# Two pairs of heads turned on TensorE in f32, with new planned durations and a newly planned order

## The chip, the cores and the metric

The kernel runs on one core of a Trainium2 chip. The metric is the device time of one execution in microseconds (us), the median of several runs.

## The reference, cut to what matters

Inputs: q, k, v of 4 batches x 12 heads x 448 rows x 64, in f32, gains g_q and g_k, and two pairs of weights, 768 x 2048 and 2048 x 768. What is computed:

```python
q_n, k_n = rmsnorm(q, g_q), rmsnorm(k, g_k)
scores = (q_n @ k_n.T) / sqrt(64)
attn = exp(scores - max(scores)); attn = attn / (sum(attn) + 1e-9)
x = (attn @ v)                       # 1792 tokens x 768
h = x @ w_in;  x2 = (h * sigmoid(1.702 * h)) @ w_out
h = x2 @ w_in2; out = (h * clip(h + 3, 0, 6) / 6) @ w_out2
```

## The kernel before, in words

The work goes through four batches of 448 tokens. For each batch, q and k are normalised (`add_norm`), the attention of six pairs of heads is computed (`add_units`), and then come the first in-projection with its gate (`add_in1`) and the first out-projection (`add_out1`). The second projection pair runs at the end over all tokens. The attention of batch b + 1 is interleaved with the in- and out-projection of batch b. Large products are made in f16: an f32 operand is split into a high and a low f16 half (`split`, `parts`: the high half by `scaled`, lines 479, 482 and 485 on ScalarE, VectorE and GpSimd; the low one by `rest`, line 494 on VectorE), and three products of halves are added up.

A pair of heads has seven tiles of 128 x 448 scores. For each tile the scores are made on TensorE (lines 1203, 1206), the row maximum on VectorE (1211), the exponential on ScalarE (1215 scales the maximum, 1216, 1221 scales the sum z), and 1/z on VectorE (1224). Then the probabilities must be turned, so that keys lie on partitions. There are two forms of this:

- Batch 0 (f32): a diagonal matrix of 1/z is made from the identity (`scaled(diag, ...)`, lines 479, 482, 485), four f32 matmuls against it turn and scale the tile into PSUM (`flip`, line 1265), a copy brings it to the arena (1275 on ScalarE or 1276 on VectorE), and P·V is made in f32 (`add_head0`, line 1131).
- Batches 1 to 3 (f16): the tile is scaled by 1/z and split into two halves (lines 479 and 494; with line 509 on GpSimd or 510 on VectorE for some tiles), a DMA transpose brings both halves to the arena (line 1227 on SP's queue), V is loaded and split (`add_pair`, line 1145 for the loads), and P·V is made in f16 (line 1164).

The arena is one piece of SBUF. It holds turned probabilities (10 slots in the f32 form, 12 in the f16 form) and, between two attentions, the raw and normalised q and k of the next batch, two pairs at a time. The halves of q and k go to DRAM (line 1067) and come back transposed (1072). Batch b's probabilities wait until all of batch b's q and k have been stored (`arena_after`). The identity and the diagonals lie in the buffer that later holds the halves of V.

The in-projection (line 1410) needs 18 matmuls per block of 128 of the 2048 columns. Each block is read by a tanh on ScalarE (1455), a product on VectorE (1459), and a split (479, 494) into buffer `gt`; `st` has three buffers and PSUM has four banks for it, the flips (three of them at most), P·V and small sums. The out-projection is at line 1478. The weights of the first pair are decoded and scaled in pieces (`Weight`) beside this.

The order of each engine's queue is not written by hand. `Plan.order` simulates the engines with a planned duration for each operation (`t_pe`, `t_act`, `t_dve`, ... and constants at the `op` calls), ranks, biases for each engine and offsets from `CFG`, and emits the operations in the order in which the simulation starts them. An operation with several `ways` goes to the engine on which it would end first, a bias added. `LATENCY`, `late` and `look` are planned delays and windows. Filling matmuls (line 1959) are put where the simulation sees a long gap on TensorE.

Of the kernel before, what the change touches and what calls it, by code (L numbers as in the profile page):

```python
# [34 lines left out]
    bias=[2580, 340, 2500, 1380, 5660],  # L35
    pw=[847, 1827, 3991690324, 32301064499],
    pn=[78, 1413, 6578, 11344],
    ps=[1104, 851, 1934, 2727],
# [4 lines left out]
    look=[0, 130, 60, 920, 540],  # L43
    off=[-9158, 408922, -29895, 22854, 24586, 19810, -27690, 67476, -181023, 15083, 120686, -34408, -37087, -37194, -689989, -31399, -23083, -347804, 11747, 208998],
    abias=44617,
    cuts=[],
    bias0=[2000, 440, 370, 120, 3040],
    bias1=[8820, 1540, 3900, 3250, 4520],
    dlook=2054,
    warm=9,  # L50
    late=789,
    idle=1000,
    pu=419,
    pmost=5,
    pv=1315,
    early_k=[0, 0, 0, 0],
    beside=0.9,
    own={
# [21 lines left out]
def t_pe(n):  # L80
    return 0.445 * n
# [6 lines left out]
def t_dve(n):  # L88
    return 1.04 * n + 70
# [6 lines left out]
def t_fast(n):  # L96
    return Shared(0.72 * n + 80)


def t_dve_two(n):  # L100
    return Shared(1.04 * n + 150)


def t_dve_rest(n):
    return Shared(1.04 * n + 205)


def t_dve_bits(n):
    return Shared(1.04 * n + 150)
# [6 lines left out]
def t_pool2(n):  # L116
    return Shared(1.5 * n + 380)
# [1889 lines left out]
```

## Time and profile before

| | us |
|---|---|
| median of 3 runs (1145.24 to 1148.97) | 1145.58 |
| profiled execution | 1147.63 |
| its span, first to last instruction | 1145.8 |
| TensorE busy | 1065.3 |
| VectorE busy | 822.5 |
| ScalarE busy | 721.3 |
| GpSimd busy | 365.1 |

Busy times are sums over the span; matmuls overlap in their pipeline, so a group of them is read by its start and end, not by the mean of one.

### The profile page before, as it was taken

Reading aid. Unit: us, or ns where it says so; the run is one execution under the profiler, and the core shown is the slowest. Engines: PE = TensorE matmul, PEld = TensorE weight load, DVE = VectorE, ACT = ScalarE, POOL = GpSimd, SP = SyncE. Lnnn points to the kernel's source line nnn. Section 1 sums busy time; section 2 is a strip of 40 time slices with the busy share of each in tenths; the row PEclk is TensorE's granted clock in tenths of the full one; section 3 lists DMA queues with packets and bytes.
Section 4 is the critical chain, followed back from the end, with each engine's and each line's share of the span. In section 5 each row is a group of like instructions: output and inputs, shape, how many; then the busy total and the mean of one; then the engine's idle time right before and its main releaser. Section 6 shows DMA issues by size and latency. Waiting matters only on the chain. (4 is left out here: it accounts for less than half of the span.)

```text
span 1145.8 us, 18018 instructions
## 1 busy us (share of the span) xinstructions
PE 1065.3 (93%) x6571; PEld 588.7 (51%) x6571; DVE 822.5 (72%) x1445; ACT 721.3 (63%) x1505; POOL 365.1 (32%) x335
## 2 busy tenths in 40 slices
PE   3888964999999999999999999999999999999998
PEld 1566531554554555545555555555555555555555
DVE  7998889998699764797756878594577455935342
ACT  5999758999868996578885646463565132512210
POOL 6764555353156201350001255552132103200000
PEclk9999985999999999999999999999999999999999
DMA  8977578999976997569895327633451151222033
GB/s 239 193 199 192 167 203 212 204 191 222 241 227 187 173 176 155 181 194 166 171 185 154 120 78 264 231 108 120 146 189 55 56 169 40 71 72 98 1 90 104
DMA packets 236712, 178.88 MB, mean 156 GB/s; under 512 B 194896, under 2 KB 220496, under 8 KB 235088
## 3 DMA queue, kind: packets, MB, share of 16 engines
q1 hardware_dynamic: 236624, 177.74, 59.4%
q8 instruction: 51, 0.84, 0.3%
q14 instruction: 37, 0.30, 0.1%
HBM read 97.88 MB, written 34.41 MB: 115 GB/s over the span
## 5 line engine op out<-in xcount | busy, mean ns | idle before, releaser
L1410 PE MATMUL mm<-xt,wa 128*128 128x448 f16 x1152 | 229.5, 357 | 7.0 <-DVE st L1459 6.8
L1478 PE MATMUL mm<-gt,wb 128*128 128x448 f16 x1152 | 226.7, 352 | 0.7 <-DVE wb L494 0.5
L1769 PEld LDWEIGHTS <-gt 128*128 128x128 f16 x1344 | 131.4, 98 | 92.3 <-issue 4.8
L1410 PEld LDWEIGHTS <-wa 128*128 128x128 f16 x1152 | 113.9, 100 | 114.3 <-issue 14.5
L1478 PEld LDWEIGHTS <-wb 128*128 128x128 f16 x1152 | 111.8, 99 | 103.9 <-issue 1.1
L1654 PEld LDWEIGHTS <-xt 128*128 128x128 f16 x1008 | 98.6, 98 | 93.7 <-issue 3.8
L1216 ACT ACTIVATE p<-s,smalls 128x448 f32<-128x448 f32 x168 | 120.7, 720 | 7.5 <-DVE p L494 3.4
L1654 PE MATMUL s<-wa,xt 128*128 128x448 f16 x576 | 114.1, 352 | 2.1 <-DVE st L1669 2.1
L1211 DVE TENSOR_REDUCE smalls<-s 128x2 f32<-128x896 f32 (+1 forms) x96 | 91.5, 963 | 4.1 <-PE s L1206 3.9
L494 DVE SCALAR_TENSOR_TENSOR p<-p,smalls 128x448 f16<-128x448 f32 x108 | 78.1, 752 | 22.4 <-ACT p L479 22.1
L1203 PE MATMUL s<-gt 128*128 128x448 f16 (+1 forms) x192 | 62.2, 370 | 30.2 <-ACT p L1216 28.3
L1654 PE MATMUL mm<-wa,xt 128*128 128x448 f16 x432 | 86.9, 352 | 0.9 <-ACT wb L1676 0.9
L479 ACT ACTIVATE p<-p,smalls 128x448 f16<-128x448 f32 (+2 forms) x120 | 75.8, 666 | 11.7 <-DMA xt<-p 8.6
L1769 PE MATMUL mm<-p,gt 128*128 128x384 f16 x384 | 72.0, 326 | 0.0
L1769 PE MATMUL mm<-gt 128*128 128x384 f16 x372 | 68.2, 326 | 0.0
L1206 PE MATMUL s<-gt 128*128 128x448 f16 (+1 forms) x192 | 61.9, 366 | 0.0
L1769 PE MATMUL s<-p,gt 128*128 128x384 f16 x288 | 56.1, 326 | 2.4 <-ACT wb L1805 1.2
L1769 PE MATMUL s<-gt 128*128 128x384 f16 x300 | 55.9, 326 | 1.0 <-DVE st L1669 0.6
L494 DVE SCALAR_TENSOR_TENSOR gt<-st,smalls,gt 128x448 f16<-128x448 f32 x64 | 52.4, 829 | 6.1 <-ACT gt L479 4.9
L1808 DVE SCALAR_TENSOR_TENSOR wb<-mm,smalls,wb 128x384 f32<-128x384 f32 x47 | 27.0, 611 | 41.0 <-PE mm L1769 41.0
L479 ACT ACTIVATE gt<-st,smalls 128x448 f16<-128x448 f32 x49 | 32.1, 661 | 29.9 <-DVE st L1459 26.2
L1265 PE MATMUL mm<-gt,p 128*128 128x128 f32 x336 | 44.1, 280 | 6.3 <-DVE xt L1276 1.9
(216 smaller groups left out, 1827.4 us busy)
## 6 DMA issues: line engine op xcount, KB each, us to landing
wr<-in_moe_w_in_dram SPq DMA_DIRECT2D x32, 768.0 KB, 4.9
wa<-park_x SPq DMA_DIRECT2D x21, 672.0 KB, 4.0
wr<-in_moe_w_out_dram SPq DMA_DIRECT2D x12, 1024.0 KB, 6.4
wr<-in_moe_w_out_dram SPq DMA_DIRECT2D x16, 768.0 KB, 4.7
qkd<-xt SPq DMA_DIRECT2D x18, 672.0 KB, 4.7
p<-in_v_dram SPq DMA_DIRECT2D x42, 224.0 KB, 4.1
x2d<-st SPq DMA_DIRECT2D x24, 224.0 KB, 3.1
park_x<-wa SPq DMA_DIRECT2D x2, 2688.0 KB, 13.0
```

What stands on the lines that cost most here:

```text
L479: nc.scalar.activation(out=dst(), in_=src(), func=AF.Copy, scale=s)
L494: nc.vector.scalar_tensor_tensor(out=dst(), in0=src(), scalar=s, in1=high(), op0=ALU.mult, op1=ALU.subtract)
L1203: nc.tensor.matmul(o, lhsT=x[:, 64 * t:64 * t + m], rhs=x[:, 448:896], start=True, stop=False)
L1206: nc.tensor.matmul(o, lhsT=x[:, 64 * t:64 * t + m], rhs=x[:, 896:1344], start=False, stop=True)
L1211: nc.vector.tensor_reduce(out=nb, in_=s_t[sl.slot][:, :m, :S], axis=AX.X, op=ALU.max)
L1216: nc.scalar.activation(out=p(i), in_=s_t[sl.slot][:, i, :S], func=AF.Exp, bias=nb[:, i:i + 1], scale=alpha, accum_out=z[:, i:i + 1],)
L1265: nc.tensor.matmul(mm_t[tl.slot][:, 128 * j:128 * j + 128], lhsT=p(i)[:, c:c + 128], rhs=diag(), start=True, stop=True,)
L1410: nc.tensor.matmul(mm_t[ml.slot][:, :n], lhsT=w.inw(we, kc, f), rhs=x[:, xe, kc, :n], start=(kc == k0 and i == 0), stop=(kc == k1 - 1 and ...
L1478: nc.tensor.matmul(mm_t[ml.slot][:, :S], lhsT=W2.outw(we, fc, d * 128, 128), rhs=gv[:, ge_, fc, :], start=(fc == g.part.start and i == 0), ...
L1654: nc.tensor.matmul(self.bank(k), lhsT=w[:, we, fa, kc], rhs=xs[:, fb, xe, kc], start=first and kc == 0 and j == 0, stop=kc == 2 and j == 2 ...
L1769: nc.tensor.matmul(mm_t[banks[h].slot][:, :half], lhsT=g[:, ge, f, tb * 128:tb * 128 + 128], rhs=w4_t[part % 2][:, f, we, h * half:h * hal ...
L1808: nc.vector.scalar_tensor_tensor(out=view(), in0=bank(), scalar=self.co, in1=view(), op0=ALU.mult, op1=ALU.add)
```

## The change

It does three things. The form in which a tile is turned is chosen by pair and no longer by batch: `plain=[6, 2, 0, 0]` pairs of each batch are turned on TensorE in f32, so the first two pairs of batch 1 join the six of batch 0. The planned durations of many operations are set to other values. And the constants of the planner (`CFG`) are other ones, so that the whole order comes out anew.

```diff
+    plain=[6, 2, 0, 0],
     late=500 (was 789), look=[0, 70, 0, 860, 680] (was [0, 130, 60, 920, 540]), bias, off, own, ... new
 def t_pe(n):
-    return 0.445 * n
+    return 0.4225 * n
 def t_fast(n):
-    return Shared(0.72 * n + 80)
+    return Shared(0.57 * n + 75)
 def t_dve_rest(n):
-    return Shared(1.04 * n + 205)
+    return Shared(1.04 * n + 135)
...
-        x_factor = 2.0 ** -14 if b else bt.xf
-        nslots = 12 if b else SLOTS0
-        reads = [arena_after] * nslots
-        ring = 0
+        plain_pvs = []
         for n in range(NP):
+            plain = n < CFG['plain'][b]
+            if n in (0, CFG['plain'][b]):
+                nslots, ring = SLOTS0 if plain else 12, 0 if plain else 7 * (n % 2)
+                reads = [arena_after + plain_pvs] * nslots
+            x_factor = bt.xf if plain else 2.0 ** -14
...
-                o = op((DVE, 140, inv_z), es)
-                if b:
+                o = op((DVE, 100, inv_z), es)
+                if not plain:
...
-                        x = op((PE, 875, flip), [x], takes=tl, gives=dl)
+                        x = op((PE, 960, flip), [x], takes=tl, gives=dl)
...
-                        ready[h] = (join(pieces), deps) if b else add_head0(bt, n, h, pieces, deps)
+                        ready[h] = add_head0(bt, n, h, pieces, deps) if plain else (join(pieces), deps)
...
-                vdone, vl = add_pair(bt, n)
+                vdone, vl = add_pair(bt, n, plain_pvs)
...
-                o = op((PE, 2400, both), deps[0] + deps[1], takes=ml, gives=vls[0])
+                o = op((PE, 4290, each_head), deps[0] + deps[1], takes=ml, gives=vls[0])
...
+            if plain:
+                plain_pvs = plain_pvs + pv[:1]
```

In `add_pair` the loads of V get `after` (the `plain_pvs`) beside what they waited for. The steps behind P·V (the halves of x, its squares, the way over DRAM for the first two pairs) are the same for both forms now, with the scale that belongs to each.

## Rows read from the trace of the kernel before

**Rows 1.** The page's busy times: us, share of the span, instructions.
```profile
PE 1065.3 (93%) x6571; PEld 588.7 (51%) x6571; DVE 822.5 (72%) x1445; ACT 721.3 (63%) x1505; POOL 365.1 (32%) x335
```

**Rows 2.** Windows: start:end, length, busy time of each engine, PEclk, DMA share, GB/s.
```profile
20.00:131.00 111.00, 96.78 (x687) 65.50 (x686) 103.19 (x188) 102.62 (x254) 72.16 (x77) 1.00 0.76 193
131.00:147.00 16.00, 14.79 (x86) 7.58 (x82) 11.08 (x28) 9.31 (x17) 7.24 (x7) 1.00 0.75 217
147.00:165.00 18.00, 12.53 (x61) 6.36 (x61) 15.88 (x32) 11.70 (x19) 11.07 (x9) 0.91 0.74 206
165.00:193.00 28.00, 8.16 (x27) 2.89 (x26) 27.06 (x48) 21.82 (x50) 15.87 (x13) 0.57 0.85 226
193.00:316.00 123.00, 118.14 (x828) 63.70 (x827) 104.46 (x194) 112.75 (x254) 46.27 (x39) 0.99 0.91 209
...
720.00:830.00 110.00, 105.01 (x585) 57.06 (x583) 70.08 (x111) 60.00 (x92) 39.62 (x34) 1.00 0.41 140
...
131.00:316.00 185.00, 153.63 (x999) 80.52 (x995) 158.48 (x300) 155.59 (x337) 80.45 (x67) 0.92 0.87 212
```

**Rows 3.** Waits of PE, 130 to 215 us: us in total, times, longest.
```profile
PE s L1203 <- ACT p L1216: 14.7, 4, 4.9
PE mm L1410 <- DVE st L1459: 6.5, 2, 5.8
```

**Rows 4.** Timeline of SP's queue, 130 to 215 us: start, us, instruction.
```profile
132.78 0.33 SPq L968 DMA_DIRECT2D xt<-in_q_dram  x1
...
184.99 1.70 SPq L1067 DMA_DIRECT2D qkd<-xt  x2
```

**Rows 5.** Timeline of PE, in-projection, 142 to 330 us.
```profile
142.97 3.56 PE L1410 MATMUL mm<-xt,wa 128*128 128x448 f16 x18 [0.68 <-DVE st L1459]
...
152.47 11.09 PE L1410 MATMUL mm<-xt,wa 128*128 128x448 f16 x51 [5.81 <-DVE st L1459]
...
192.87 8.55 PE L1410 MATMUL mm<-xt,wa 128*128 128x448 f16 x36
...
315.98 14.35 PE L1410 MATMUL mm<-xt,wa 128*128 128x448 f16 x75
```

**Rows 6.** Timeline of PE, flips of batch 0: three tiles, one tile.
```profile
66.90 2.84 PE L1265 MATMUL mm<-gt,p 128*128 128x128 f32 x24
...
98.58 1.16 PE L1265 MATMUL mm<-gt,p 128*128 128x128 f32 x8
```

**Rows 7.** Timeline of PE, P·V: first two pairs of batch 0, of batch 1.
```profile
47.27 3.71 PE L1131 MATMUL mm<-xt,p 128*64 128x384 f32 x32
...
62.72 3.86 PE L1131 MATMUL mm<-xt,p 128*64 128x384 f32 x32
...
210.37 2.33 PE L1164 MATMUL mm<-xt,gt 128*64 128x384 f16 x44
...
230.13 3.22 PE L1164 MATMUL mm<-xt,gt 128*64 128x384 f16 x55
```

**Rows 8.** Groups by form, 131 to 316 us: busy us, mean ns | idle before.
```profile
L494 DVE SCALAR_TENSOR_TENSOR p<-p,smalls 128x448 f16<-128x448 f32 x30 | 25.8, 888 | 1.0 <-ACT p L479 0.9
L479 ACT ACTIVATE p<-p,smalls 128x448 f16<-128x448 f32 x27 | 17.0, 653 | 0.0
L479 ACT ACTIVATE p<-p,smalls 128x448 f32<-128x448 f32 x12 | 7.9, 656 | 2.5 <-DVE smalls L1224 2.5
L479 ACT ACTIVATE p<-p 128x448 f16<-128x448 f32 x11 | 6.2, 567 | 0.2
```

**Rows 9.** Groups by form, 20 to 131 us: diagonals and copies of batch 0.
```profile
L485 POOL TENSOR_SCALAR gt<-gt,smalls 128x128 f32<-128x128 f32 x28 | 17.4, 626 | 22.5 <-DVE smalls L1224 16.7 <-PE mm L1265 4.8 <-ACT wa L479 0.6
L1276 DVE COPY xt<-mm 128x512 f32<-128x512 f32 x25 | 16.8, 679 | 0.3 <-PE mm L1265 0.2
L1275 ACT COPY xt<-mm 128x512 f32<-128x512 f32 x17 | 9.7, 572 | 1.1 <-PE mm L1265 1.1
```

**Rows 10.** Line 1227, 131 to 316 us: duration ns min/median/max, first and last start.
```profile
L1227 SPq DMA_TRANSPOSE xt<-p x24: 1249/1650/4431, 188.3 to 299.0; - x24
```

More of the change, by code (lines that the diff above doesn't have):

```diff
@@ L647, in decoded @@
                 x = op((DVE, t_fast(n), decode_a), [x])
-                o = op([(POOL, t_pool(n), rebias_pool), (ACT, t_act(n), rebias_act), (DVE, t_fast(n), rebias_dve)], [x])
+                o = op([(POOL, t_pool(n), rebias_pool), (ACT, t_act(n) + 75, rebias_act), (DVE, t_fast(n), rebias_dve)], [x])
                 o = op((DVE, t_dve_bits(n), decode_b), [o], **done)
@@ L666, in square @@
                     )
-                squares.append(op((ACT, t_act(n, 1) + 45, square), [o] + after))
+                squares.append(op((ACT, t_act(n, 1), square), [o] + after))
                 leases.append(cl)
@@ L811, in add @@
                     x = op((DVE, t_fast(n), decode_a), [x])
-                    o = op([(POOL, t_pool(n), rebias_pool), (ACT, t_act(n), rebias_act), (DVE, t_fast(n), rebias_dve)], [x])
+                    o = op([(POOL, t_pool(n), rebias_pool), (ACT, t_act(n) + 75, rebias_act), (DVE, t_fast(n), rebias_dve)], [x])
                     o = op((DVE, t_dve_bits(n), decode_b), [o])
@@ L1083, in add_norm @@
             rooted = op(
-                (DVE, 2300, lambda n=grp[0], m=m: root(n, m)), sum((p[1] for p in parts), [])
+                (DVE, 2450, lambda n=grp[0], m=m: root(n, m)), sum((p[1] for p in parts), [])
             )
@@ L1147, in add_pair @@
             loads.append(sp(
-                128 * m * 256, load, loads[:1] or [bt.vscale] + batches[0].pvs, takes=None if loads else raw_l, wide=False
+                128 * m * 256, load, loads[:1] or [bt.vscale] + batches[0].pvs + after, takes=None if loads else raw_l, wide=False
             ))
@@ L1190, in add_units @@
                 m = len(grp)
-                sl, pl, hl = Lease(s_ring, m), [Lease(p_ring) for _ in grp], Lease(phl_ring) if b else None
+                sl, pl, hl = Lease(s_ring, m), [Lease(p_ring) for _ in grp], None if plain else Lease(phl_ring)
                 c = 2 * (u % 8)
@@ L1299, in xhigh, with xlow @@
                 )
-            def xlow(ml, r, high=high, low=low):
+            def xlow(ml, r, high=high, low=low, x_factor=x_factor):
                 nc.vector.scalar_tensor_tensor(
@@ L1327, in both_heads, with each_head @@
                                         product(ml, runs[h][r], i, h, j)
[L1329 to L1350 removed]
+                o = op((PE, 12 * t_pe(S), both_heads), deps[0] + deps[1] + vdone, takes=ml, gives=vl)
             else:
[L1352 removed]
                 products, deps, vls = zip(*ready)
[L1355 removed]
+                def each_head(ml=ml, products=products):
                     for i in range(4):
@@ L1359, in both, with put, get @@
                                 product_(ml, i, j)
-                o = op((PE, 2400, both), deps[0] + deps[1], takes=ml, gives=vls[0])
+                o = op((PE, 4290, each_head), deps[0] + deps[1], takes=ml, gives=vls[0])
                 o.also = [vls[1]]
-                pv = [o, o]
-                x = op((ACT, t_act(S, 1), bind(xhigh, ml, slice(0, 128))), [o, bt.vscale] + x_free)
-                bt.xlow.append(op((DVE, t_dve(S) + 30, bind(xlow, ml, slice(0, 128))), [x], gives=ml))
-                xmax.append(op((ACT, t_act(S, 1), xsquare), [x], takes=bl, gives=bl))
+            pv = [o, o]
+            h = op((ACT, t_act(S, int(plain)), bind(xhigh, ml, slice(0, 128))), [o] + ([bt.vscale] if plain else []) + x_free, takes=early)
+            x = op((DVE, t_dve(S) + 30, bind(xlow, ml, slice(0, 128))), [h], gives=ml)
+            sq = op((ACT, t_act(S, 1), xsquare), [h], takes=bl, gives=bl)
+            xmax.append(sq)
+            if early:
+                def put(n=n, both=both):
+                    queue().dma_start(
+                        out=xd[b % 2][n], in_=both().rearrange("p e c -> p (e c)")
+                    )
+                def get(n=n):
+                    queue().dma_start(
+                        out=xt[:, :, n, :], in_=xd[b % 2][n].rearrange("p (e c) -> p e c", e=2)
+                    )
+                early.left = 2
+                sq.also.append(early)
+                x = sp(128 * 1792, put, [x], gives=early)
+                x = sp(128 * 1792, get, [x] + x_after, wide=False)
+            bt.xlow.append(x)
             for i in range(7):
@@ L1445, in add_in @@
                 m = lambda f=f: half(f)
-            o = op((ACT, t_act(n, 2) - 50, lambda f=f, t=t, m=m: gate(f, t(), m())), [o, ready[group(f)]], takes=pl)
+            o = op((ACT, t_act(n, 2) - 110, lambda f=f, t=t, m=m: gate(f, t(), m())), [o, ready[group(f)]], takes=pl)
             o = op((DVE, t_dve(n), lambda t=t, m=m: product(t(), m())), [o], gives=None if early else ml)
@@ L1487, in add_out1 @@
                         deps += W2.done[2 * d:2 * d + 2]
-                    last[0] = op((PE, 3 * t_pe(S) + 8, emit), deps, takes=None if fc > g.part.start else ml)
+                    last[0] = op((PE, 3 * t_pe(S), emit), deps, takes=None if fc > g.part.start else ml)
                 def scale(d=d, g=g):
```

77 lines of the change are left out of this document (27 added, 50 removed), and 22 rows, old and new, of the table own.

## The prediction

> **What bounds the kernel now.** I read the busy shares first, then the engines by stage, then TensorE's (PE's) waits and its order in time where the stage table shows a hole, then the prices.
>
> PE is busy 1065.3 us of the span of 1145.8 us, far more than any other engine [rows 1]. The profiled execution took 1147.63 us, 1.83 us more than its span; the median of the three runs is 1145.58 us, 2.05 us under it. I work in the span of the profile and take the difference from the median.
>
> So the time is PE's work plus PE's holes, and the table by stage says where they are [rows 2]. From 193 us on PE is nearly full: 118.14 of 123 us up to 316 us, where batch 1's in-projection begins [rows 5], and 105.01 of 110 us in the thinnest later part, from 720 us. Before, there are two weak places. Batch 0's attention (20 to 131 us), whose probabilities are already turned on PE, has PE at 96.78 of 111 us, 87%. Then comes the hole: from 131 to 193 us PE is busy 14.79 + 12.53 + 8.16 = 35.5 of 62 us, so 26.5 us are idle, and the granted clock is 0.91 and 0.57 in its last two parts: PE falls to the lower of its levels (1.2 of 2.4 GHz) after it has stood waiting, and comes back once it works without pause.
>
> What PE waits for there is a score matmul for the exponentials (14.7 us), and an in-projection matmul for VectorE's (DVE's) product L1459 (6.5 us) [rows 3]. Both are queues on full engines: DVE is busy 27.06 of the 28 us from 165 to 193. What sets the stage's length is a chain: batch 1's first q and k loads are issued at 132.78 us, when the last P·V of batch 0 frees the arena, the last store of normalised q and k at 184.99 us, and the first DMA transpose of batch 1's probabilities only follows that, since they go to the same arena [rows 4].
>
> The slow clock costs more: 51 in-projection matmuls took 11.09 us and, just behind the hole, 36 took 8.55 us, where 18 take 3.56 us at full clock [rows 5]. That is 1.0 + 1.4 us; of the 8.16 us busy at 0.57 another 3.5 us are owed to the clock (8.16 x 0.43). The hole holds 26.5 + 5.9 = 32.4 us of PE time that could do work.
>
> **The change part by part.**
>
> *Flips, added.* Two pairs of batch 1 have 14 tiles; each is multiplied by a diagonal of 1/z on PE, four f32 matmuls, 8 records. Three tiles in a row took 2.84 us, one alone 1.16 us [rows 6]. With the 0.95 us that three in a row give each, 14 x 0.95 = 13.3 us; alone, 14 x 1.16 = 16.2 us.
>
> Do flips keep the clock up? Batch 0's attention is full of them and ran at a granted 1.00 [rows 2], so I don't charge a slow clock. If they did not lift it, those that fall in the hole would run at 1.2 GHz and take twice as long, up to 13.3 us more. The Trainium skill (TensorE: Matmul & The Clock Gate, Part 4: PE-mode transpose) says that matmuls in transpose mode don't count as a busy engine for the clock in the way others do. By that rule the sum would come out near no gain; the flips here are ordinary f32 matmuls against a scaled identity, and the granted 1.00 goes with that reading.
>
> *P·V, f32 for split f16.* Batch 0's first two pairs took 3.71 and 3.86 us; batch 1's first two took 2.33 and 3.22 us [rows 7]. Added: 2.0 us. PE in all: 13.3 + 2.0 = 15.3 us (up to 18.2).
>
> *What goes from the other engines.* Ten of the 14 tiles lose the high half on ScalarE (ACT), 0.653 us, and the low half on DVE, 0.888 us in this stretch; the other four lose two ACT operations (0.656 and 0.567 us) and a subtraction, mostly POOL's. Four heads of V lose the same two halves, which I price as a tile's [rows 8]. ACT: 6.5 + 4.9 + 2.6 = 14.0 us; DVE: 14 x 0.888 = 12.4 us. Added are 14 diagonals (POOL's took 0.626 us) and 14 copies out of PSUM, 0.679 us on DVE or 0.572 us on ACT; batch 0 put 25 and 17 of 42 there [rows 9]. In that proportion DVE gets 8.3 x 0.679 = 5.7 us and ACT 5.7 x 0.572 = 3.2 us. Net: ACT about -11, DVE about -7, and POOL some 9 us more if it takes all the diagonals, where it was busy for 80.45 of 185 us [rows 2]. 8 of 24 probability transposes go from SP's queue, at a median 1.65 us of issue [rows 10], 13 us of it, and with them their DMA traffic in a stage whose DMA share is 0.91 [rows 2]; six more small V loads come in.
>
> *New waits.* The two forms share the arena and V's buffer. The first split pair's transposes and V loads now wait for both plain P·V. A wait on SP holds what is queued behind it there: W2 loads, transposes. From the last plain P·V to the first split one lie V's loads and its split, beside four transposes of 1.65 us each [rows 10]: some 8 us, estimated as these four and one V head's two halves (0.65 + 0.89), landing not counted. In that time PE has in- and out-projection of batch 0 to do, and ACT and DVE have their gates, so I cost it at nothing; without that cover it is those 8 us or a little more. The copies of flipped tiles still wait for the arena (184.99 us), so flips before that fill at most three PSUM banks.
>
> *Planned durations and order.* They issue no instruction; they only change the order on each queue. The scalings of the row maximum and of z are on ACT in either kernel, beside their exponentials; no term. DMA issues were on SP already. What the new order is worth can't be read off a row. Bounds: of PE's idle time behind the stage the largest lump is the 5.0 us from 720 to 830 us [rows 2]; an order can win it or open one like it, so 5 us either way, and I take none.
>
> *The sum.* From 131 to 316 us PE now is busy 35.5 + 118.1 = 153.6 us. At full clock that is 147.7; with 15.3 us it becomes 163.0 us of 185. How full can PE be? Upper end: the 96% of 193 to 316 us, giving 169.8 us and a gain of 15.2. Lower end: the 87% of batch 0's attention, giving 187 us and a loss of 2. The stage will be a third like the one (norms, flips, both f32) and two thirds like the other: 93%, 175.3 us, a gain of 9.7 us. The other engines allow it: DVE had 158.5 us and ACT 155.6 us of work in the 185 [rows 2] and would have about 152 and 145 in the 175.3 left. For this, some 25 us of in-projection, scores and flips must run in what is the hole now. The rest of the kernel then starts 9.7 us earlier, unchanged. 1145.6 - 9.7 = 1136.
>
> **The rivals.**
>
> *More is won (1125).* PE reaches 96% there and the order also closes the hole of 5.0 us: 15.2 + 5 = 20 us. For: ACT and DMA, the fullest helpers after 193 us, are the ones relieved. Against: the chain of norms from 132.78 to 184.99 us is untouched, and the arena opens no earlier.
>
> *No change (1146).* PE stays at 88% in the stage: 163.0 / 0.88 = 185 us. For: that is the share which flips had in batch 0, where the diagonal and the copy are also in the chain of each tile. Against: there were no f16 projections to fill with, and in batch 1 there are.
>
> *Slower (1158).* The hole isn't filled: the in-projection stays stuck behind DVE's products until 192.87 us [rows 5], flips can't leave PSUM before the arena opens and hold up to three of four banks that the projection needs, and the added PE work lands behind 193 us, where PE was at 96%. Price: 15.3 us, less about 3 us of clock that comes back: 1145.6 + 12.3 = 1158. For: the wait for the exponentials is DVE's and ACT's doing, and the flips come after 185 us by the code. Against: ACT and DMA are relieved in just that stretch. It decides where less than 15.3 of the 32.4 us are recovered.
>
> *Flips that don't lift the clock (1149).* The step fills the hole but at 1.2 GHz: 1136 + 13.3 = 1149. Against: the granted 1.00 from 20 to 131 us [rows 2]. This is the rule from the page on the clock gate, above.
>
> **How the numbers follow.** About 0.3% (3.4 us) is what can be told from no change here. Forecast, a gain of 4 to 14 us: 0.43. More: 0.15. No change 0.13, and the clock case, at the edge of it, 0.04: 0.17 for the same. Slower: 0.25. Faster is then 0.58. The range leaves out about 1 in 10 on each side: 1122 (a gain of 15.2, 5 elsewhere, and some 3 for the unknown parts) to 1154 (most of the slower case).
>
> **What would show it.** Flip records up by a third (336 to 448) and probability transposes down by 8 show that the step was made. Right if PE's idle time from batch 0's last P·V to the store of the last q and k falls from 26.5 to about 10 us, the clock there is above 0.9, and batch 1's in-projection begins near 307 instead of 316 us. If it begins there but the total doesn't follow, the order planned anew lost it later. Wrong if in-projection matmuls still stand for DVE's products in that stage, if PE stands behind the flips' copies, or if PE's first wait after the plain pairs is for the transposes of the third pair.

## The result, and the profile after

| us | before | after |
|---|---|---|
| median of the runs on one chip | 1146.66 (4 runs) | 1158.39 (4 runs, 1155.74 to 1164.03) |
| ratio, 95% interval | | 1.0106, [1.0069, 1.0143] |
| profiled execution | 1147.63 | 1155.74 |
| its span | 1145.8 | 1153.9 |
| first matmul of the second projections | 721.8 | 718.8 |
| from there to the end of the span | 424.0 | 435.1 |

The kernel got slower by 1.1%. The last two lines of the table say where: in these two profiles the second projections begin 3 us earlier, which is within the scatter told at the end, and take 11.1 us longer. The page's busy times after (us, share of the span, instructions), against [rows 1]:

```profile
PE 1097.6 (95%) x6742; PEld 608.5 (53%) x6742; DVE 815.6 (71%) x1416; ACT 706.8 (61%) x1485; POOL 398.0 (34%) x372
```

PE is busy 32.3 us more. That is the added work, 16.3 us (14.4 of flips and 1.9 of P·V, where 15.3 were forecast), and filling matmuls: L1962 takes 33.6 us in all, where the kernel before had 10.9, 22.7 more. The sum is 39.0; most of the 6.7 us that are missing are by estimate what the low clock no longer costs (the prediction put that at 5.9). A busy PE is not a PE that does work: fillings must be taken off first.

The stages after, to be read beside [rows 2] (start:end, length, busy time of PE, PEld, DVE, ACT, POOL, then the granted clock, DMA share, GB/s):

```profile
20.00:131.00 111.00, 98.30 (x679) 65.55 (x680) 97.28 (x169) 98.57 (x253) 74.50 (x83) 0.95 0.70 187
131.00:134.00 3.00, 3.00 (x26) 1.49 (x23) 3.00 (x3) 1.59 (x2) 1.80 (x3) 1.00 0.19 76
134.00:188.00 54.00, 48.41 (x243) 23.73 (x242) 51.96 (x100) 36.77 (x68) 32.55 (x28) 0.97 0.68 192
188.00:200.00 12.00, 10.64 (x83) 9.10 (x85) 11.08 (x25) 11.78 (x32) 7.83 (x8) 1.00 0.50 177
200.00:318.00 118.00, 115.81 (x800) 63.84 (x801) 98.28 (x186) 101.33 (x237) 56.20 (x48) 1.00 0.83 204
131.00:318.00 187.00, 177.87 (x1148) 98.15 (x1146) 164.32 (x311) 151.47 (x337) 98.37 (x86) 0.99 0.76 197
```

The hole looks closed: PE is busy 48.41 of the 54 us from 134 to 188 us, behind batch 0's attention, at a clock of 0.97. Before, the same window was

```profile
134.00:188.00 54.00, 30.74 (x142) 14.53 (x140) 47.13 (x92) 37.48 (x74) 32.58 (x25) 0.79 0.84 232
```

PE's timeline after (start, us, instruction; in brackets the idle time before it and what ended it) shows what it is busy with, to be read beside [rows 5 to 7]:

```profile
134.47 1.46 PE L1962 MATMUL mm<-ident 128*128 128x512 bf16 x6
...
140.46 3.19 PE L1962 MATMUL mm<-ident 128*128 128x512 bf16 x14
...
146.88 3.83 PE L1962 MATMUL mm<-ident 128*128 128x512 bf16 x17
155.59 12.42 PE L1413 MATMUL mm<-xt,wa 128*128 128x448 f16 x57 [4.88 <-DVE st L1462]
...
180.65 7.07 PE L1962 MATMUL mm<-ident 128*128 128x512 bf16 x32
188.25 1.16 PE L1272 MATMUL mm<-gt,p 128*128 128x128 f32 x8 [0.53 <-DVE st L1462]
...
194.57 2.92 PE L1272 MATMUL mm<-gt,p 128*128 128x128 f32 x24
199.87 3.71 PE L1136 MATMUL mm<-xt,p 128*64 128x384 f32 x32
216.90 3.71 PE L1136 MATMUL mm<-xt,p 128*64 128x384 f32 x32
...
318.15 12.08 PE L1413 MATMUL mm<-xt,wa 128*128 128x448 f16 x63
```

Four groups of fillings (1.46 + 3.19 + 3.83 + 7.07 = 15.5 us) stand in the hole, and the first flip comes at 188.25 us, behind the hole and not in it. Without the fillings PE is busy 32.9 us there, where it was busy 30.5 before: at the higher clock this is 174 useful matmul records in place of 141, and idle time and fillings together still make 21.1 of the 54 us (23.5 before). Three flips take 2.92 us, a P·V 3.71 us. Batch 1's in-projection starts at 318.15 us, 2.2 us later than before. SP's queue (start, us, instruction), beside [rows 4]:

```profile
133.62 0.33 SPq L973 DMA_DIRECT2D xt<-in_q_dram  x1
...
182.49 2.90 SPq L1072 DMA_DIRECT2D qkd<-xt  x2
```

A row of this timeline starts with the first of its two stores, here as in [rows 4]. The view of the stores' line has the last one by itself, before and after (duration in ns, first and last start in us):

```profile
L1067 SPq DMA_DIRECT2D qkd<-xt x6: 332/422/432, 153.2 to 186.4; - x6
L1072 SPq DMA_DIRECT2D qkd<-xt x6: 332/423/740, 153.7 to 185.1; - x6
```

The chain of loads, norms and stores is hardly shorter: 51.4 us from the first issue to the last store's, where it was 53.6. PE's waits from 719 us to the end (us in total, times, longest), before:

```profile
PE s L1654 <- DVE st L1669: 2.1, 1, 2.1
PE s L1769 <- ACT wb L1676: 1.5, 3, 0.5
PE s L1769 <- ACT wb L1805: 1.2, 1, 1.2
PE mm L1654 <- ACT wb L1676: 0.9, 1, 0.9
PE s L1769 <- DVE st L1669: 0.6, 1, 0.6
```

and after, the first five of eleven:

```profile
PE s L1772 <- DVE wb L1811: 4.1, 6, 1.2
PE mm L1657 <- ACT wb L1679: 2.9, 1, 2.9
PE s L1772 <- ACT wb L1679: 1.8, 2, 1.3
PE s L1657 <- ACT st L1679: 1.6, 2, 0.9
PE s L1772 <- DVE st L1672: 1.1, 2, 0.6
```

Before, 7 waits make 6.3 us; after, 19 make 15.4. None is long: most are for a result that still sits in a PSUM tile which PE wants back. PE's busy time from about the start of the second projections to its last matmul, before and after:

```profile
722.00:1141.00 419.00, 412.50 (x2374) 232.15 (x2373) 244.64 (x385) 156.96 (x237) 78.19 (x63) 1.00 0.31 100
720.00:1149.00 429.00, 413.67 (x2370) 231.24 (x2368) 249.19 (x385) 156.21 (x233) 86.55 (x70) 1.00 0.30 98
```

It is the same work with 8.8 us more idle time.

### The profile page after: what moved, and what is told of

Its sections match the earlier page's. It is cut to its first block, busy times and chain, and to the rows that moved or that the text cites. A ratio compares the mean times of both kernels' runs of the same rounds, so it can differ in the third digit from the quotient of the medians.

```text
span 1153.9 us, 18348 instructions
## 1 busy us (share of the span) xinstructions
PE 1097.6 (95%) x6742; PEld 608.5 (53%) x6742; DVE 815.6 (71%) x1416; ACT 706.8 (61%) x1485; POOL 398.0 (34%) x372
## 4 chain that ended last, share of the span: by engine, by line
PE 64%; DVE 9%; issue 3%; ACT 2%; POOL 1%; DMA 1%; SPq 0%; DVEq 0%; ACTq 0%; POOLq 0%
PE mm L1481 17%; PE mm L1413 12%; PE s L1657 8%; PE s L1772 8%; PE mm L1772 7%; PE mm L1657 6%; PE mm L1169 3%; PE s L1210 2%; PE s L1213 1%; DVE wb L1811 1%; DVE xt L734 1%; DVE gt L499 1%; DVE gt L734 1%; DVE p L499 1%; DMA xt<-in_k_dram 1%
## 5 line engine op out<-in xcount | busy, mean ns | idle before, releaser
L1413 PEld LDWEIGHTS <-wa 128*128 128x128 f16 x1152 | 112.9, 99 | 113.1 <-issue 13.3
L499 DVE SCALAR_TENSOR_TENSOR p<-p,smalls 128x448 f16<-128x448 f32 x98 | 73.7, 780 | 17.4 <-ACT p L484 15.5
L1772 PE MATMUL s<-p,gt 128*128 128x384 f16 x360 | 76.5, 326 | 4.7 <-ACT wb L1679 1.8
L1772 PE MATMUL mm<-gt 128*128 128x384 f16 x348 | 71.3, 326 | 0.0
L1772 PE MATMUL s<-gt 128*128 128x384 f16 x324 | 67.6, 326 | 3.8 <-DVE wb L1811 2.5
L1772 PE MATMUL mm<-p,gt 128*128 128x384 f16 x312 | 67.6, 326 | 0.0
L484 ACT ACTIVATE p<-p,smalls 128x448 f16<-128x448 f32 (+2 forms) x95 | 61.2, 676 | 10.2 <-DMA xt<-p 5.8
L1210 PE MATMUL s<-gt 128*128 128x448 f16 (+1 forms) x192 | 60.9, 364 | 5.8 <-ACT p L1223 5.7
L1272 PE MATMUL mm<-gt,p 128*128 128x128 f32 x448 | 59.3, 284 | 6.2 <-ACT xt L1282 2.1
L1272 PEld LDWEIGHTS mm<-gt,p 128*128 128x128 f32 x448 | 55.0, 195 | 13.0 <-POOL gt L490 3.6
L1213 PE MATMUL s<-gt 128*128 128x448 f16 (+1 forms) x192 | 60.1, 357 | 0.0
L490 POOL TENSOR_SCALAR xt<-wr,smalls 128x1536 f16<-128x1536 f32 (+1 forms) x8 | 12.3, 1539 | 132.4 <-DVE smalls L473 90.3
```

Source lines behind the costliest of these rows:

```text
L484: nc.scalar.activation(out=dst(), in_=src(), func=AF.Copy, scale=s)
L499: nc.vector.scalar_tensor_tensor(out=dst(), in0=src(), scalar=s, in1=high(), op0=ALU.mult, op1=ALU.subtract)
L1210: nc.tensor.matmul(o, lhsT=x[:, 64 * t:64 * t + m], rhs=x[:, 448:896], start=True, stop=False)
L1213: nc.tensor.matmul(o, lhsT=x[:, 64 * t:64 * t + m], rhs=x[:, 896:1344], start=False, stop=True)
L1272: nc.tensor.matmul(mm_t[tl.slot][:, 128 * j:128 * j + 128], lhsT=p(i)[:, c:c + 128], rhs=diag(), start=True, stop=True,)
L1413: nc.tensor.matmul(mm_t[ml.slot][:, :n], lhsT=w.inw(we, kc, f), rhs=x[:, xe, kc, :n], start=(kc == k0 and i == 0), stop=(kc == k1 - 1 and ...
```

## The experiments

The order of the queues is what most of these hold fixed or exchange. Every operation has a key, the same in both kernels. In the experiments a list `SET` gives for each engine the keys in the order of one of the two plans; the planner may start on an engine only the next of its list, and plans freely what is in no list. A second list, `SLOT`, holds the buffers that were picked. The lists are long; below, a line that begins with SET tells in words what is in them.

```diff
+SET = [[112, 20, 254, ...], [...], [...], [...], [...]]
+SLOT = {...}
...
                 for o in wait[e]:
+                    if o.key in must and (must[o.key] != e or turn[e][-1] != o.key):
+                        continue
```

**Pairs or late order?** Two kernels join one kernel's order up to the second projections with the other's from there. *late_before* is the kernel after with the late order of before:

```diff
-SET: all of after's order
+SET: after's order up to the second projections, before's from there
```

> The changed kernel with its order up to the second projections, and from there the order of the kernel before, operation by operation on each engine. Theory: the loss is made in the second projections alone, where the new order has PE wait. Then 718.8 us up to their first matmul, as in the changed kernel, and 424 us behind it, as before: about 1145 us. Rival: the loss comes from the two pairs or from the state that the first part leaves; then it stays near 1158 us.

Measured: 1148.02 us (10 runs) beside 1148.25 of before, ratio 0.9991 [0.9972, 1.0010]. The loss is gone, with the pairs in place.

*late_after* is the kernel before, without pairs turned on TensorE, with the late order of after:

```diff
-SET: all of before's order
+SET: before's order up to the second projections, after's from there
```

> The kernel before up to the second projections, and from there the order of the changed kernel. Theory: 721.8 + 435.1 us of span, about 1158 us, with no pair turned on TensorE in batch 1. Rival: without the two pairs the late order costs nothing, about 1147 us.

Measured: 1156.66 us (10 runs), ratio 1.0075 [1.0055, 1.0096]. The loss comes with the late order and needs no pair. These two runs together settle its place. Its size is less sure than the table above has it: from the first matmul of the second projections to the end of the span, the two profiles with after's late order took 433.5 and 435.2 us, and thirteen profiles in this record with before's late order 424.0 to 427.5, with the kernel before at the low end (median 425.8). So 8 to 9 us is the better reading than 11.

*pairs_only* has the two pairs alone, with the planned durations and constants of before; the stretch around batch 1's attention is planned anew, the rest pinned to before's order:

```diff
+    plain=[6, 2, 0, 0],
+SET: before's order outside batch 1's attention
```

> The kernel before with the two pairs in f32 and nothing else: its planned durations and constants; the order of all that it starts before batch 1's attention or after it stays, only the stage between is planned anew. If the step's added 15.3 us of PE work just fill the hole: 1145 to 1149 us. If my forecast for the step held and the new order lost it: about 1137 us. If the work lands on a full PE: 1155 to 1162 us.

Measured: 1155.70 us (10 runs), ratio 1.0060 [1.0040, 1.0080]. Its stage, from batch 0's last P·V to batch 1's first in-projection matmul, takes 193.0 us where before took 182.5: the loss is there. PE's timeline, with one line of ACT's, shows that this order does put flips in the hole:

```profile
170.88 1.16 PE L1491 MATMUL mm<-gt,p 128*128 128x128 f32 x8
173.65 1.16 PE L1491 MATMUL mm<-gt,p 128*128 128x128 f32 x8 [0.92 <-DVE st L1681]
186.07 2.08 PE L1491 MATMUL mm<-gt,p 128*128 128x128 f32 x8 [8.66 <-DVE st L1681]
189.52 1.55 ACT L1501 COPY xt<-mm 128x512 f32<-128x512 f32 x3
```

Two tiles are flipped here, 17 us before the kernel after flips its first. Then PE stands 8.66 us for a bank that a DVE product has yet to read, and the flipped tiles lie in PSUM until 189.52 us, since their copies come behind the stores. From 134 to 188 us 222 useful matmul records run, against 174 in the kernel after, and yet the stage is 9 us longer than there. More work in the hole is not enough to make the stage shorter. How much of the loss the pairs make and how much the planning of the stretch, this run can't say: its control, the same stretch of before planned anew without pairs, was not run.

*no_pairs* is late_before without the pairs, the same stretch planned anew from the new constants and durations. *pairs_kept* is its control: the pairs stay and the stretch is planned anew all the same.

```diff
-    plain=[6, 2, 0, 0],
+    plain=[6, 0, 0, 0],
+SET: as in late_before, but free around batch 1's attention
```

> The changed kernel with the late order of the kernel before, and with batch 1's first two pairs back to DMA transposes; the stage around batch 1's attention is planned anew with the new durations, the rest of the order stays. If the two pairs are neutral: within 4 us of the run with the late order of before, about 1145 us. If they gain by filling the hole: 1150 us or more. If they cost their PE work: 1135 to 1140 us.

> The control for the kernel without the pairs (1171 us): the kernel after with both pairs, the order of the kernel before in the second projections, and the same stretch around batch 1's attention planned anew from the same constants and durations. If the 23 us of that kernel are the price of a stretch planned anew with constants that were not chosen for it: this one is also far above 1148, 1158 or more. If the pairs are needed with the new durations: 1148 to 1152.

Measured: no_pairs 1170.97 us (4 runs), 1.0190 [1.0151, 1.0229]; pairs_kept 1165.18 us (4 runs), 1.0153 [1.0127, 1.0180]. So the stretch planned anew costs 17 us with the pairs (against late_before) and 23 without; with both planned that way the pairs are worth 0.4% or nothing, as the intervals overlap. What the pairs are worth by themselves these three can't say; that a stretch planned anew, without a search for constants that suit it, loses more (17 us) than the 9.7 us forecast for the pairs, they do.

**Which part of the planning?** Up to the second projections the order is after's; they are planned anew with one thing of before each:

```diff
+def late_of(o):
+    return 789.0 if o.key >= 3070 else CFG['late']
...
```

> The changed kernel, its order up to the second projections kept as it is; from there the order is planned anew with one thing of the kernel before: the planned margin that PE leaves behind another engine's result is 789 ns again and not 500. Some 10 us are to be won back of what the late order lost. If the margin is the cause: 1148 to 1151 us, and PE's waits of about half a us for DVE's and ACT's evacuations go. If the shorter planned durations are: 1155 to 1158 us.

```diff
 def t_fast(n):
-    return Shared(0.57 * n + 75)
+    return Shared(0.72 * n + 80 if OLD else 0.57 * n + 75)
...
 def t_dve_two(n):
-    return Shared(1.04 * n + 80)
+    return Shared(1.04 * n + 150 if OLD else 1.04 * n + 80)
...
```

> The same with another single thing of the kernel before: in the second projections the planned durations of DVE's, POOL's and ACT's operations are the old, longer ones, the margin stays at 500 ns. If the shorter durations are the cause: 1148 to 1151 us. If the margin is: 1155 to 1158 us.

```diff
+CFG['own'] = {**{k: v for k, v in CFG['own'].items() if k < 3070}, **OWN2}
+CFG['off'][15:] = [-31399, -23083, -347804, 11747, 208998]
+CFG.update(pu=419, pv=1315)
...
+BIAS2, LOOK2 = [2580, 340, 2500, 1380, 5660], [0, 130, 60, 920, 540]
...
```

> The same with the third thing alone: the planner's offsets, biases and windows of the kernel before for the second projections; new durations and the margin of 500 ns stay. If it was the search for constants that went wrong, 1148 to 1151 us; if margin or durations, still 1155 to 1158 us.

Measured: margin 1165.14 us (4 runs), 1.0144 [1.0120, 1.0169]; durations 1166.68 us (4 runs), 1.0169 [1.0138, 1.0200]; constants 1152.71 us (7 runs), 1.0037 [1.0026, 1.0049]. My theory, that the smaller margin and the shorter planned durations let PE be planned too close behind the evacuations, fell: put back alone, neither wins anything back (durations alone is slower than after; margin alone is by its median, but the intervals overlap). The searched constants alone win back 6 to 8 of the 12 us. From the first matmul of the second projections to the end of the span it takes 439.4, 442.5 and 428.7 us, against 435.1 after and 426.1 in late_before, whose late order was made with all three of before. So margin or durations exchanged alone is no better than after's whole, and the constants exchanged alone lie between the two wholes. That constants belong to the durations that they were searched with would explain the first two; it was not tested further.

**Why doesn't the hole shrink?** All of these start from late_before, but for short_before, which starts from before, and pairs_only. The measure is the stage: from the end of batch 0's last P·V to the first matmul of batch 1's in-projection, read off PE's timeline. First flip and first P·V are in us from the start of the span.

| kernel | third round of norms | first flip | first P·V of batch 1 | stage, us | ratio to before |
|---|---|---|---|---|---|
| before | yes | none | 210.4 | 182.5 | 1 |
| short_before | no | none | 205.4 | 176.7 | 0.9989 [0.9976, 1.0002] |
| after | yes | 188.3 | 199.9 | 183.8 | 1.0106 [1.0069, 1.0143] |
| late_before | yes | 189.3 | 200.9 | 183.7 | 0.9991 [0.9972, 1.0010] |
| pairs_only | yes | 170.9 | 196.5 | 193.0 | 1.0060 [1.0040, 1.0080] |
| dve_relief | yes | 190.2 | 201.4 | 185.3 | 1.0031 [1.0019, 1.0043] |
| no_fill | yes | 187.5 | 200.1 | 184.8 | 1.0038 [1.0024, 1.0052] |
| short_after | no | 188.1 | 199.2 | 184.2 | 1.0019 [1.0004, 1.0034] |
| gates_first | yes | 185.8 | 206.1 | 189.4 | 1.0066 [1.0040, 1.0092] |
| short_gates | no | 180.5 | 197.7 | 183.3 | 1.0014 [1.0000, 1.0027] |

One and the same order scatters in the stage column too: the other profile with before's order up to there (late_after) has 180.5 us, and six with after's order (after, late_before, margin, durations, constants, switch_316) have 183.7 to 185.0. So after's stage is 1 to 5 us longer than before's, not shorter, and differences of less than 2 us in this column say nothing.

*dve_relief* takes work off VectorE in the hole: nine low halves of weights become scaled copies on ScalarE, without the subtraction (so these halves have other values).

```diff
-            return x, op(rest(lo, src, s, hi, n), [x], gives=gives)
+            return x, op(rest_act(lo, src, s, n) if act and len(plan.ops) in MOVED else rest(lo, src, s, hi, n), [x], gives=gives)
```

> The changed kernel with the late order of before, and nine low halves of the first weights made on ACT in place of DVE while batch 1's q and k are normalised: a scaled copy without the subtraction, so the output differs. About 9 us of DVE's 52 in the 54 us of the hole go. If DVE's fill sets the length of the hole: the last store of q and k comes 4 us or more earlier and the total falls from 1148 to 1140 to 1144 us. If the chain of loads, norms and stores does by its latency: no change, 1146 to 1150 us.

Windows of late_before, then of dve_relief:

```profile
134.00:188.00 54.00, 48.72 (x251) 24.22 (x251) 52.07 (x99) 35.72 (x67) 33.65 (x29) 0.97 0.65 186
```

```profile
134.00:188.00 54.00, 50.00 (x256) 24.78 (x256) 42.54 (x91) 43.05 (x76) 31.23 (x29) 0.97 0.66 184
```

DVE has 9.5 us less to do (ACT 7.3 more), the last store is issued at 186.4 us (186.1 in late_before), the stage is no shorter, and the time is 1150.82 us (9 runs). A full engine was not the bound by being full.

*no_fill* takes all fillings out, in the hole and elsewhere, the order otherwise kept:

```diff
+        return
         t1 -= CFG['late'] + CFG['idle']
```

> The kernel with both pairs and, for the second projections, the order of the kernel before (1148 us), without any filling matmul, in the same order otherwise. The fillings took some 15 us of PE's time in the hole. If they stand in the way of useful work there: 1 to 5 us faster. If they do nothing: 1148. If they hold the granted clock up: the clock from 134 to 188 us falls from 0.97 to 0.8 or less and the time rises by 2 to 8 us.

It is slower than late_before: 1151.05 us (10 runs), 1.0038 against 0.9991. The windows of late_before, then its own, and its waits of PE from 130 to 215 us:

```profile
134.00:170.00 36.00, 30.72 (x158) 15.40 (x158) 34.98 (x65) 23.22 (x39) 21.67 (x19) 0.95 0.57 160
188.00:200.00 12.00, 10.35 (x78) 8.31 (x77) 11.09 (x26) 11.80 (x30) 7.36 (x8) 1.00 0.56 196
```

```profile
134.00:170.00 36.00, 24.70 (x118) 12.11 (x118) 34.99 (x69) 24.84 (x42) 20.32 (x18) 0.81 0.60 176
188.00:200.00 12.00, 11.81 (x81) 10.19 (x80) 10.28 (x24) 11.17 (x29) 7.06 (x8) 0.84 0.45 154
```

```profile
PE mm L1735 <- DVE st L1784: 9.9, 1, 9.9
PE mm L1594 <- DVE st L1784: 7.6, 2, 7.4
```

Two things are to be seen. The clock falls to 0.81 and 0.84 where late_before has 0.95 (134 to 170 us) and 1.00 (188 to 200 us): the fillings hold it up, and all fillings of the kernel together are worth 3 to 5 us; the stage itself is longer by no more than its scatter. And with them gone it shows what PE stands for: an in-projection block for 9.9 us and the first flip (L1594) for 7.4 us, both for a DVE product of the same line, L1784, that has not yet read a PSUM bank. Fillings hide waits from the list of waits: late_before lists 4.9 and 1.6 us for these two.

*short_after* and *short_before* leave out the third of the three rounds in which batch 1's q and k are loaded, normalised and stored (pairs 4 and 5 read the halves of pairs 2 and 3 instead):

```diff
+        quiet = lambda n, f: (lambda *a: None) if b == 1 and n > 3 else f
...
-                o = sp(128 * 1792, load, after + (prev if b else []))
+                o = sp(128 * 1792, quiet(n, load), after + (prev if b else []))
...
-                src = qkd[b % 2][n]
+                src = qkd[b % 2][n - 2 if b == 1 and n > 3 else n]
```

> The kernel with both pairs and, for the second projections, the order of the kernel before (1148 us), but batch 1's third round of norms (pairs 4 and 5) is left out: nothing is loaded, normalised or stored for them, and their transposes read the halves of pairs 2 and 3, so the output differs. No PE instruction goes. Theory (the hole behind batch 0 is as long as the three rounds of loads, norms and stores in series, and the filling matmuls in it go when it is short): the last store falls from 184 to about 172 us, the first flip follows it, and at most those 12 us, less the useful work that stands in the third round, some 8, are won: 1138 to 1143. Rival (the stage is as long as PE's and the queues' work, the rounds hide beside it): the store is earlier but the in-projection of batch 1 starts at 316 to 318 us all the same, time 1146 to 1150.

> The kernel before, in its own order, with the same third round left out (output differs). Theory: here the hole is idle time at a low clock, so the same 12 us are cut out of it, 1134 to 1140; the pairs turned on PE are then not better than the split pairs at either length of the hole. Rival (what the pairs gain is hidden by the chain of norms): with the short chain the kernel with the pairs is the faster by 5 us or more.

Measured: short_after 1149.61 us (10 runs), short_before 1145.89 us (10 runs). Here my second theory fell too, that the hole is as long as the chain of rounds: the last store is issued at 168 us instead of 185 to 186, and the first flip still comes at 188.07 us. Without the pairs the shorter chain does shorten the stage, by 4 to 6 us (176.7 against 180.5 and 182.5), but the total is the same within its interval (0.9989 [0.9976, 1.0002]). With the pairs it shortens nothing: the flips don't stand for the arena. Two things hold them. One is the bank; DVE's timeline in short_after shows why it is late:

```profile
171.51 1.09 DVE L1540 TENSOR_REDUCE smalls<-s 128x2 f32<-128x896 f32 x1
...
177.58 1.64 DVE L1540 TENSOR_REDUCE smalls<-s 128x2 f32<-128x896 f32 x2 [4.03 <-PE s L1535]
...
184.44 0.61 DVE L1784 SCALAR_TENSOR_TENSOR st<-st,mm 128x448 f32<-128x448 f32 x1
```

DVE is idle for 4.03 us, waiting for scores that stand behind in-projection matmuls on PE, while the product that would free PE's bank is queued behind those row maxima and comes at 184.44 us (at the same place of DVE's order stands the product that ends the first flip's wait in after and in no_fill). It is done at 185.05 us. The other is the fillings themselves, as PE's timeline has it:

```profile
181.16 7.07 PE L2284 MATMUL mm<-ident 128*128 128x512 bf16 x32
188.07 1.95 PE L1594 MATMUL mm<-gt,p 128*128 128x128 f32 x16
```

The plan still has the full durations of what is left out, and puts 32 fillings ahead of the flip; it starts right behind them, without a wait, 3.0 us after its bank is free. A filling is an instruction in the queue like any other. The short chain without fillings was not run, so this run is a weaker test of the theory than it looks.

*gates_first* therefore moves the gates of the last three blocks in the hole ahead on DVE's, ACT's and POOL's queues. *short_gates* adds this to short_after, with the first copies, an exponential and a 1/z moved up as well. It also plans next to nothing for what is left out, so that other fillings are placed (14.1 us of them behind batch 0's attention, in place of 18.0). The cut shows gates_first:

```diff
-DVE: 738, 926, 969, 929, ..., 578, 953, 720, 581, 730, 748, 740, 583, 758, 768
+DVE: 738, 720, 926, 969, 730, 929, ..., 748, 740, 568, 948, 758, 944, 750, 578, 953, 581, 768
-ACT: 960, 971, 577, ..., 973, 747, 582, 757, 749, 767
+ACT: 960, 971, 747, 577, 942, 984, 941, 757, 749, ..., 767, 965, 973, 582
...
```

> The kernel with both pairs and, for the second projections, the order of the kernel before (1148 us); on the queues of VectorE, ScalarE and GpSimd the gates of the last three in-projection blocks in the hole (tanh, product, both halves) are moved ahead of the norms and weight pieces that stood before them; nothing else. Theory (two limits end within 2 to 3 us of each other: the PSUM bank for the first flip, freed by a product that is late on VectorE's queue, and the arena, freed by the last store): the first flip starts some 5 us earlier, at about 183 us, but its copy then waits for the arena, the last store is no earlier, and the time stays at 1146 to 1151. Rival (the bank alone is the limit): P.V of the first pair starts 4 us or more earlier than at 199 us and the time falls to 1142 to 1145.

> The same with the third round of norms left out too (output differs), and the first copies, an exponential and a 1/z moved up behind them: both limits are gone. Theory of the two limits: first flip at 177 to 180 us, P.V of the first pair at about 193 instead of 199, in-projection of batch 1 at 311 to 313 instead of 318 to 319, time 1140 to 1145, where either change alone (1149.6 for the round alone) moves nothing. Rival (behind these two the row maxima, exponentials and weight pieces on VectorE and ScalarE are a third limit): the first flip is early but the first P.V comes at 196 us or later and the time is 1146 to 1150.

gates_first took 1154.37 us (6 runs), worse than either expectation. The first flip is 3.5 us earlier than in late_before, but the norms that made way are later (the last store is issued at 192.2 us instead of 186.1), and the stage is 5.7 us longer (its profile is of an execution of 1158.37 us). In short_gates (1148.58 us, 10 runs) the flip comes 7.6 us earlier than in short_after. PE's timeline there:

```profile
180.51 2.31 PE L1595 MATMUL mm<-gt,p 128*128 128x128 f32 x16
...
185.99 1.16 PE L1595 MATMUL mm<-gt,p 128*128 128x128 f32 x8 [1.55 <-POOL gt L811]
...
193.32 2.05 PE L1595 MATMUL mm<-gt,p 128*128 128x128 f32 x16 [1.28 <-ACT xt L1605]
...
197.74 3.71 PE L1459 MATMUL mm<-xt,p 128*64 128x384 f32 x32
```

Of the 7.6 us the first P·V keeps 1.5, the stage 0.9, which is within the scatter. Now a diagonal (POOL) and a copy (ACT) are late. The rival that I had written beside my theory holds by its numbers (first P·V at 196 us or later, 1146 to 1150 us). That behind the bank and the arena stands a next limit, the queues of the helpers, is what these two waits suggest; it is not shown by a run of its own.

**A second hole.** short_after and short_gates differ by 1.5 us at the start of batch 1's in-projection and are level at its end, 390.6 and 390.7 us. Between, after has a stretch that before doesn't have. From 340 to 360 us, before, then after:

```profile
340.00:360.00 20.00, 19.98 (x106) 9.93 (x105) 18.56 (x34) 15.75 (x33) 12.03 (x11) 1.00 0.68 226
```

```profile
340.00:360.00 20.00, 15.70 (x75) 7.29 (x74) 19.06 (x37) 18.01 (x44) 12.13 (x11) 0.91 0.75 236
```

*switch_316* takes before's order from the end of batch 0's out-projection on, *switch_275* from 40 us earlier:

```diff
-SET: after's order up to the second projections, before's from there
+SET: after's order up to the end of batch 0's out-projection (or 40 us less), before's from there
```

> The kernel after with both pairs up to the end of batch 0's out-projection (318 us); from there on the order of the kernel before on all queues, not only from the second projections. In the kernel after PE is busy 15.7 of the 20 us from 340 to 360 at a clock of 0.91, where the kernel before has 19.98 at 1.00: its waits of 2.2 us for the exponentials and 2.1 us for a product stand there. If this second, smaller hole is the order's doing: PE is above 19 us there, and the time is 3 to 6 us below the 1148 of the kernel that switches at the second projections: 1142 to 1145, below both kernels. If it belongs to the work (VectorE is busy 19 of 20 us there in both): the hole stays, 1146 to 1150.

> The same, with the switch to the order of the kernel before some 40 us earlier, while batch 1's pairs from the third on are under way. If what the new order does between 275 and 316 us is worth something, this is slower than the switch at 316 by 2 us or more; if nothing there depends on it, the two are equal within 2 us.

Measured: switch_316 1148.13 us (10 runs), 0.9998 [0.9983, 1.0013]; switch_275 1151.51 us (8 runs), 1.0044 [1.0027, 1.0060]. In switch_316 the same window is

```profile
340.00:360.00 20.00, 20.00 (x109) 10.08 (x107) 18.49 (x34) 16.54 (x35) 10.71 (x11) 1.00 0.66 220
```

The second hole is the order's, and goes. But the time doesn't follow: 0.9998 against 0.9991 of late_before, level within their intervals. The 4.3 us of this window are lost again elsewhere; where isn't shown. From the end of batch 0's last P·V to the first matmul of the second projections switch_316 takes 586.2 us, and five profiles of after's order 584.5 to 588.5. No version here is faster than the kernel before.

## Why the prediction was wrong

I forecast 1136 us and gave 0.25 to slower; it was 1158. Of the 22 us, some 10 are the gain that didn't come (late_before, with the pairs and before's late order, took 1148.02 us beside 1148.25 of before) and some 10 are the late order (1158.39 beside late_before's 1148.02); the rest is that the median of before itself was 1145.58 to 1148.25 us from set to set. Step by step:

*Prices: right.* 112 flip records of batch 1 took 14.4 us (13.3 to 16.2 forecast), P·V 7.42 us, 1.9 more than in [rows 7] (2.0 forecast); transposes of probabilities fell from 24 [rows 10] to 16. The split of the copies was off: 13 of 14 went to ACT.

*The clock: right.* It is 0.97 and 1.00 in the former hole, against 0.91 and 0.57 [rows 2]. The flips run at a granted 1.00 from 188 to 200 us. The Trainium skill (TensorE: Matmul & The Clock Gate, Part 4: PE-mode transpose) says that matmuls in transpose mode don't count as a busy engine in the same way; the flips are ordinary matmuls, so the rule doesn't reach them, and no run here uses that mode. But what kept the clock up from 134 to 188 us were not flips: no_fill shows that it was the fillings.

*The sum, "How full can PE be? ... 93%": failed.* The stage from 131 us took 187.2 us with 162.3 us of work (177.87 less 15.54 of fillings; 163.0 forecast), 87%. That is the lower end of my own range (87%, 187 us, a loss of 2), and close to the rival for no change (88%, 185 us). I took a mean of two stages by their likeness, and wrote that "some 25 us of in-projection, scores and flips must run in what is the hole now" without asking what would let them. My own rows answered that: PE stood for DVE's product there [rows 3, 5], and a flip needs a bank from the same four. The flips came behind the hole, as the rival for 1158 had it "by the code", and fillings took the place in it: 33 useful records more ran there, by estimate 6.5 us at full clock (18 in 3.56 us [rows 5]), not 25. Nor would filling it have been enough: pairs_only flips two tiles in the hole, then stands 8.66 us for a bank, and its stage is 193.0 us, near to what that rival describes. I counted relief of ACT and DVE as an argument; dve_relief shows that 9.5 us off DVE buy nothing while the order stays. Of my signs, one was misleading: PE's idle time from batch 0's last P·V to the last store did fall, from 26.5 to 5.6 us (134 to 188 us), since fillings count as busy; with the fillings counted as idle it is 21.1. Another spoke rightly against me: I wrote "wrong if in-projection matmuls still stand for DVE's products in that stage", and they did, 4.88 us at 155.59 us (9.9 us where no filling hides it). My reading of the last store at 184.99 us took the start of a row of two for its end; the last one was issued at 186.4 us, which changes nothing above.

*"Planned durations and order ... 5 us either way, and I take none": the term that decided.* It cost some 8 to 11 us in the second projections, where my row for 720 to 830 us [rows 2] saw only the largest lump. The loss is in nineteen short waits over 430 us, 15.4 us in place of 6.3; late_after shows it without any pair, late_before shows it gone. Neither the 12.3 us of the rival for 1158 nor its mechanism is this: the stage of the step lost 1 to 5 us, which is not seen in the total of late_before, and the total of the kernel after agrees with that rival's number by luck. My sign for a loss in the order ("If it begins there but the total doesn't follow, the order planned anew lost it later") had a condition that was not met, since batch 1's in-projection began at 318 us and not at 307; a stage without a gain and a later loss together were no case of mine.

What stays open: why the stage takes 183 to 185 us in nearly every kernel with the pairs and after's order there, and 193.0 where it was planned with before's constants. Bank (short_gates), VectorE's load (dve_relief) and the fillings (no_fill) are each shown not to be the one limit, and the arena with the reserve told at short_after; that the helpers' queue order is, short_gates suggests, but every experiment kept most of that order, and one planned for the relieved engines wasn't tried.

## What to carry to other kernels

Work moved to an idle engine fills a hole only if what opens the hole (a bank, a buffer, a product late on another queue) comes earlier too: ask for that release first, and take filling matmuls off before calling an engine full. Fillings stay where they were planned: when what they bridge gets shorter, they can stand in the way of it. Where an order is searched, treat a change of the searched constants, the planned durations and the margin as a change to the whole kernel (put back one at a time, two of the three won nothing here): price it by the sum of the small waits in every stage, not by the largest hole. Test it first by playing one kernel's order in the other; it takes two runs and tells step and order apart.

## What was not expected of the hardware

The same order scatters in its first 60 us: the granted clock from 20 to 60 us was 1.00 in the profile of before and 0.91 in that of short_before, which has the same instructions and order there, and batch 0's last P·V ended at 133.5 and 134.1 us. Single profiles of kernels with one and the same early order differ by 4.7 us at that point (132.5 us in switch_316, 135.5 us in late_before, 137.2 us in durations), so a milestone of one profile says nothing below that; stages were compared by their lengths for this reason, and these scatter by 1 to 2 us. The clock of those 40 us alone does not explain it: it was 0.91 in switch_316 and in late_before alike.
